# Moving VectorE work between two K stages of a transformer block: query sums earlier, layer-norm statistics on two engines, a block's transposing loads on two queues

## The chip, the cores and the metric

The kernel runs on one core of one Trainium2 chip. The metric is the device time of one execution in microseconds (us). Each of the core's engines has its own instruction queue and works through it strictly in order: TensorE (PE in the profile) multiplies matrices, VectorE (DVE) and ScalarE (ACT) do elementwise work, GpSimd (POOL) does small elementwise work and issues some DMAs, and SyncE (SP) issues DMAs only. An instruction waits at the head of its queue until what it needs is there, and all that stands behind it waits too.

## The reference, cut to what matters

```python
def phi(t): return where(t > 0, t + 1, exp(t)) + 1e-6

mod = (silu(c) @ w_mod)                   # six rows of 512: sa, ca, ga, sb, cb, gb
h = layernorm(x) * (1 + ca) + sa          # x: 2048 x 512
q, k, v = split(h @ wqkv)                 # 32 heads of 16
pq, pk = phi(q), phi(k)
kv, z = pk^T v, sum of pk                 # per head
x = x + ga * ((pq kv / (pq z + 1e-6)) @ wo)
h = layernorm(x) * (1 + cb) + sb
x = x + gb * (mish(h @ w1 + b1) @ w2)     # 512 -> 1792 -> 512
```

All is float32. Everything in this study happens in the second and third line of it: the layer norm of x, its transposition, and the keys.

## The kernel before

**Tiling.** The 2048 rows are four blocks of 512 (b = 0 to 3), and a block is four tiles of 128 x 512. A float32 operand is multiplied as two rounded parts, a high half and a low half (`split`, L80): ScalarE copies the value to the high half, one tick later VectorE subtracts it from the value and gets the low half. `mm3` (L74) is then three matmuls (high x high, high x low, low x high, L76 to L78).

**Normalised and transposed x.** TensorE needs h with the model dimension on the partitions. Blocks 0 and 1 are transposed by TensorE. Blocks 2 and 3 (`TURNED`) go another way: `ln_turned` (L487) normalises the four tiles in place and writes them to DRAM (`to_dram`); `load_squares` (L256) reads them back in small pieces of 32 floats, 16 DMAs a block, four for each tile `y_x`, so that squares of 32 x 32 lie in the right place; VectorE transposes within the squares (`turn`, L267), ScalarE applies scale and shift of the modulation (L269), and `split` makes `hT`. In `ln_turned`, a tile's mean and variance come either from ScalarE (`act_sums`, L221: two passes with accumulation) or from VectorE (`ln_stats`, L192: one statistics and one aggregating operation). Then one power on POOL (L207) gives the reciprocal deviations of all four tiles, VectorE makes the shifts (L237), and each tile is normalised (L216 on ScalarE, L218 on VectorE).

**Keys.** For each block b there are two loops of four units (L847 and L865). `k_unit(b, t)` makes the keys of one tile of rows: 12 matmuls with `hT` of block b. Its followers (`k_post`, L305) take the exponential and the ReLU on ScalarE, join them on VectorE (`ku`, L303), and split them (`pk`). For blocks 1 and 2 a POOL DMA also adds `ku` onto the tile of block 0 (L312), for block 3 VectorE does (L310). `xn_split` splits the normalised tile. `g_unit(b, t)` multiplies it with `pk` into `gacc`, again 12 matmuls. The stage of the "second K" is that of b = 1. The prediction calls these units K1.0 to K1.3, G1.0 to G1.3, K2.0 and so on. After G3.2 comes `z` (L359), which sums the joined `ku` tiles.

**Queries.** The queries of blocks 0 and 1 are made later with seven products instead of eight (`q_sevens`). They need sums of the transposed x of these two blocks: `q_right(c)`, c = 0 and 1, does four subtractions on VectorE, two to a step, and splits the four results one after the other; `q_left(c)` does the like with the weights.

**What sets the order.** Nothing is scheduled by a compiler: instructions enter the queues in the order in which the program calls them. Followers are Python generators. `spawn` adds one, and `tick()` (L59), called behind each unit, runs every generator up to its next `yield`, in the order in which they were spawned. Generators given to `spawn_idle` come last in each tick, and only the first `width[0]` of their list take a step; `width[0]` is 2 in this stretch. So whatever a tick puts on VectorE stands ahead of all that a later tick puts there. In the second loop the transposes of `turn_x` are called at t = 1 and t = 2 ahead of the unit and its tick. SBUF tiles of 128 x 512 share 101 slots.

In the kernel before, `ln_turned(2, 2, 2, sp)` is spawned ahead of G0.3 and `ln_turned(3, 4, 1, pool)` (all four tiles' sums on ScalarE, one tile a tick) at K1.1; `q_right(0)` and `q_right(1)` are spawned behind G1.2 and G1.3.

Of the kernel before, what the change touches and what calls it, by code (L numbers as in the profile page):

```python
# [13 lines left out]
P = 128  # L14
# [13 lines left out]
def block_kernel(ctx: ExitStack, tc: tile.TileContext, x, wqkv, wo, w1, b1t, w2, c, wmodt, out):  # L28
    nc = tc.nc
    act, dve, pool, pe, sp = nc.scalar, nc.vector, nc.gpsimd, nc.tensor, nc.sync  # L30
# [9 lines left out]
    def sb(name, dt=F32, shape=(P, 512)):  # L40

        return big.tile(list(shape), dt, tag="T", name=name, bufs=SLOTS)
# [7 lines left out]
    running, fresh, idle_work, width = [], [], [], [2]  # L50

    def spawn(gen):
        fresh.append(iter(gen))

    def spawn_idle(gen):

        idle_work.append(gen)
# [22 lines left out]
    def split(name, t, keep, key, lo_engine=dve, hi_engine=act, plus=None):  # L80

        hi, lo = sb(f"{name}h", F32R, t.shape), sb(f"{name}l", F32R, t.shape)
        if hi_engine is act:
            act.activation(hi, t, AF.Copy)
        else:
            hi_engine.tensor_copy(hi, t)
        if lo_engine is dve:
            yield
        if plus is None:
            lo_engine.tensor_tensor(lo, t, f32(hi), op=ALU.subtract)  # L90
        else:
            dve.scalar_tensor_tensor(lo, t, plus, f32(hi), op0=ALU.add, op1=ALU.subtract)
        keep[key] = hi, lo


    xt, wm, wraw = {}, {}, {}
# [95 lines left out]
    def ln_stats(key, b, j, t):  # L192

        for d, name, shape in (mv, "mv", [P, 4, 2]), (rs, "rs", [P, 4]), (nb, "nb", [P, 4]):
            if (key, b) not in d:
                d[key, b] = cst.tile(shape, F32, tag=name, name=f"{name}_{key}_{b}", bufs=NB)
        st6 = cst.tile([P, 6], F32, tag="st6", name=f"st6_{key}_{b}_{j}", bufs=4)
        dve.bn_stats(st6, t)
        dve.bn_aggr(mv[key, b][:, j, :], st6)

    def ln_eps(key, b, lo=0, hi=4):
        dve.tensor_scalar(rs[key, b][:, lo:hi], mv[key, b][:, lo:hi, 1], EPS, 1.0, op0=ALU.add, op1=ALU.mult)  # L202

    def ln_rstd(key, b, lo=0, hi=4):

        y = rs[key, b][:, lo:hi]
        pool.tensor_tensor(y, y, half[:, lo:hi], op=ALU.pow)  # L207

    def ln_shift(key, b, lo=0, hi=4):

        dve.scalar_tensor_tensor(nb[key, b][:, lo:hi], mv[key, b][:, lo:hi, 0], -1.0, rs[key, b][:, lo:hi],
                                 op0=ALU.mult, op1=ALU.mult)

    def ln_apply(key, b, j, t, dst, engine):
        if engine is act:
            act.activation(dst, t, AF.Identity, bias=nb[key, b][:, j:j + 1], scale=rs[key, b][:, j:j + 1])  # L216
        else:
            engine.tensor_scalar(dst, t, mv[key, b][:, j, 0:1], rs[key, b][:, j:j + 1],  # L218
                                 op0=ALU.subtract, op1=ALU.mult)

    def act_sums(key, b, t, v):  # L221

        if (key, b) not in rs:
            for d, name in (rs, "rs"), (nb, "nb"):
                d[key, b] = cst.tile([P, 4], F32, tag=name, name=f"{name}_{key}_{b}", bufs=NB)
        scrap = sb(f"scrap_{key}_{b}_{t}")
        sums = cst.tile([P, 2], F32, tag="sums", name=f"sums_{key}_{b}_{t}", bufs=6)
        act.activation(scrap, v, AF.Identity, scale=-1.0 / D, accum_out=sums[:, 0:1])
        act.activation(scrap, v, AF.Square, bias=sums[:, 0:1], accum_out=sums[:, 1:2])
        return sums  # L230
# [5 lines left out]
    def sums_shift(key, b, t, sums):  # L236
        dve.tensor_tensor(nb[key, b][:, t:t + 1], sums[:, 0:1], rs[key, b][:, t:t + 1], op=ALU.mult)  # L237
# [4 lines left out]
    nd, yd = {}, {}  # L242
# [6 lines left out]
    def squares(y, d, col):  # L249

        for c in range(4):
            lo = col + 32 * c
            yield (y[32 * c:32 * (c + 1), :].rearrange("q (m r) -> q m r", r=32),
                   d[:, lo:lo + 32].rearrange("(m q) r -> q m r", q=32))

    def load_squares(key, b, order=(0, 2, 1, 3)):  # L256


        for j in order:
            y = yd[key, b, j] = sb(f"y_{key}_{b}_{j}")  # L260
            for sq, rows_ in squares(y, nd[key, b], P * j):
                sp.dma_start(sq, rows_)

    def turn(key, b, j, keep, name, sc0, sh0):

# [120 lines left out]
    def q_right(c):  # L386

        b11, b12, b21, b22 = [hfx.pop((b, k)) for k in (c, c + 2) for b in (0, 1)]
        t = [sb(f"qt_{c}_{i}") for i in range(4)]
        for n, (d, u, v) in enumerate(((t[0], b12, b11), (t[1], b22, t[0]), (t[2], b22, b12), (t[3], b21, t[1]))):  # L390
            dve.tensor_tensor(d, u, v, op=ALU.subtract)
            if n % 2:
                yield
        for i in range(4):
            yield from split(f"qt_{c}_{i}", t[i], qb, (f"t{i + 1}", c))
# [88 lines left out]
                        plus_one(16, 20)  # L484
            yield

    def ln_turned(b, on_act, per, queue):  # L487

        sums = {}
        rest = list(range(on_act, 4))  # L490
        for n in range(max(on_act, len(rest))):
            if n < on_act:
                sums[n] = act_sums("x", b, n, xt["x", b, n])
            if n < len(rest):
                ln_stats("x", b, rest[n], xt["x", b, rest[n]])
            if (n + 1) % per == 0:
                yield
        for n in range(on_act):
            dve.tensor_scalar(rs["x", b][:, n:n + 1], sums[n][:, 1:2], 1.0 / D, EPS, op0=ALU.mult, op1=ALU.add)
        if rest:  # L500
            ln_eps("x", b, on_act, 4)
        ln_rstd("x", b)
        yield
        for n in range(on_act):
            sums_shift("x", b, n, sums[n])
        for pair in (0, 2), (1, 3):
            for j in pair:
                ln_apply("x", b, j, xt["x", b, j], xt["x", b, j], act if j < on_act else dve)
            if per == 1:
                yield  # L510
            for j in pair:
                to_dram("x", b, j, xt["x", b, j], queue)
        if b == 2:
            yield
            load_squares("x", b, range(4))

    def stats(b, t):
        ln_stats("x", b, t, xt["x", b, t])
# [144 lines left out]
        for j in range(4):  # L663
            load_x(b, j)
    g_unit(0, 2)
    spawn(ln_turned(2, 2, 2, sp))
    tick()
    for j in range(4):
        tr = transpose("x", 1, j, 4, 0, "h" if j < 3 else "tp", pool)
# [175 lines left out]
    for b in range(1, NB):  # L845
        last = b == NB - 1
        if b == NB - 2:  # L847
            spawn(mod_side(range(8, 12), 1))
        for t in range(4):
            k_unit(b, t)  # L850
            if b == 1 and t == 1:
                spawn(ln_turned(3, 4, 1, pool))
            if b == 2 and t == 3:
                load_squares("x", 3, range(4))
            if b == NB - 2:
                load_wqkv(0, t)
            if last and t < 2:
                spawn_idle(q_left(t))
            if last and t == 2:
                spawn_idle(early_rows[0])  # L860
            xn_split(b, t)
            tick()
        if last:
            spawn(wo_scale())
        for t in range(4):  # L865
            if b + 1 in TURNED and t in (1, 2):
                for j in (2 * t - 2, 2 * t - 1):
                    tr = turn_x(b + 1, j)
                    next(tr)
                    spawn(tr)  # L870
            elif not last and b + 1 not in TURNED and t % 2 == 0:
                for j in (t, t + 1):
                    tr = transpose("x", b + 1, j, 4, 0, "tp" if j == t else "h")
                    next(tr)
                    spawn(tr)
            g_unit(b, t)
            if b == 1 and t == 2:
                spawn_idle(q_right(0))
            if b == 1 and t == 3:
                spawn_idle(q_right(1))  # L880
            if last:
                load_x(0, t, "r")
                for k in ((0, 1), (2,), (3,), ())[t]:
                    spawn(split(f"wq_{k}", wraw[0, k], wq, k))
                if t == 2:
                    z_unit()
                if t == 3:
                    spawn(z_side())
            if b == NB - 2:
                wv[t] = sb(f"wv_{t}")  # L890
                sp.dma_start(wv[t], wqkv[P * t:P * (t + 1), 1024:1536])
                wos[t] = sb(f"wo_{t}")
                sp.dma_start(wos[t], wo[P * t:P * (t + 1), :])
            tick()
# [196 lines left out]
    order = {8: [(0, 0), (0, 2)], 9: [(0, 1)], 10: [(0, 3), (1, 0)], 11: [(1, 2)], 12: [(1, 1)], 13: [(1, 3)]}  # L1091
    for b in range(1, NB):
        for t in range(4):
            n = 4 * b + t
# [162 lines left out]
    order = [(b, j) for b in (2, 3) for j in (0, 2, 1, 3)]  # L1257
# [306 lines left out]
```

## Time and profile before

| | us |
|---|---|
| median of three runs | 487.3 (486.95 to 488.3) |
| the profiled execution | 487.84 |
| its span, first to last instruction | 486.1 |
| TensorE busy | 477.5 |
| VectorE busy | 382.2 |
| ScalarE busy | 305.9 |
| POOL busy | 148.0 |

The profile is of one execution; its span leaves out what lies around the first and the last instruction. TensorE's granted clock was 1.00 throughout. In the timelines each line has the start, the duration, the engine, the source line, the operation, output and inputs, and in brackets how long the engine had been idle before it and which instruction ended that. Successive instructions of one engine overlap a little, so the distance of two starts, not the duration, is what an operation takes in a row of them.

### The profile page before, as it was taken

What the parts mean: (1) busy time and instruction counts of PE and PEld (TensorE: products, weight loads), DVE (VectorE), ACT (ScalarE), POOL (GpSimd) and SP (SyncE); (2) the same over time, 40 slices, a digit from 0 to 9 for tenths busy, and PEclk for the clock granted to TensorE, in tenths of its full rate; (3) what the DMA queues carried; (4) which work ended last, traced back from release to release, by engine and by line L of the source; (5) the groups of instructions that cost most, each with busy time, mean ns of one, the idle gap of its engine ahead of it and who ended that gap; (6) DMA issues with size and microseconds to landing.
All of it is one profiled execution on the core that took longest, in us unless ns stands there. A gap on an engine that the chain in (4) does not pass through costs nothing.

```text
span 486.1 us, 7325 instructions
## 1 busy us (share of the span) xinstructions
PE 477.5 (98%) x2326; PEld 390.8 (80%) x2326; DVE 382.2 (79%) x740; ACT 305.9 (63%) x554; POOL 148.0 (30%) x248
## 2 busy tenths in 40 slices
PE   7999999999999999999999999999999999999997
PEld 6777767878887888888888888888888888888887
DVE  6976799999799799978777673899644665689993
ACT  6797988765654888748766764684164454668400
POOL 4674321000023105102234433332726410253600
PEclk9999999999999999999999999999999999999999
DMA  8805989343984227289699989979999922499986
GB/s 302 305 1 137 191 214 233 136 133 95 319 209 113 98 56 232 95 255 357 221 319 374 362 209 208 316 229 329 340 384 359 253 58 79 110 179 234 238 127 134
DMA packets 130849, 103.80 MB, mean 214 GB/s; under 512 B 74449, under 2 KB 95961, under 8 KB 130810
## 3 DMA queue, kind: packets, MB, share of 16 engines
q1 hardware_dynamic: 99528, 57.57, 42.4%
q0 software_dynamic: 29024, 45.24, 35.8%
q10 hardware_dynamic: 2258, 0.53, 0.5%
q8 instruction: 18, 0.29, 0.2%
q14 instruction: 21, 0.17, 0.1%
HBM read 65.55 MB, written 35.66 MB: 208 GB/s over the span
## 4 chain that ended last, share of the span: by engine, by line
PE 87%; DVE 5%; DMA 2%; ACT 2%; SPq 2%; issue 1%; POOL 1%; DVEq 0%; ACTq 0%
PE p_a L1151 20%; PE p_s L1151 8%; PE oacc L76 5%; PE oacc L78 5%; PE oacc L77 5%; PE m L77 5%; PE m L76 5%; PE m L78 5%; PE o L76 3%; PE o L78 3%; PE o L77 3%; PE pq_a L409 3%; PE pq L76 2%; PE pq L78 2%; PE pq L77 1%; PE pk L78 1%
## 5 line engine op out<-in xcount | busy, mean ns | idle before, releaser
L207 POOL TENSOR_TENSOR rs_n<-rs_n,half 128x1 f32<-128x1 f32 x16 | 11.0, 687 | 63.0 <-DVE rs_n L202 35.4
L1156 DVE TENSOR_TENSOR cb<-p_s,u 128x512 f32<-128x512 f32 x28 | 19.3, 688 | 12.1 <-ACT u L1192 12.1
L1161 ACT ACTIVATE u<-p_a 128x512 f32<-128x512 f32 x14 | 8.4, 598 | 25.9 <-PE p_a L1151 25.9
L1449 POOL DMA_DIRECT2D wt_m<-w2t x20 | 14.0, 704 | 32.8 <-PE p_a L1151 21.4
L1186 ACT ACTIVATE u<-p_a 128x512 f32<-128x512 f32 x12 | 7.2, 598 | 25.8 <-PE p_a L1151 25.8
L1143 ACT ACTIVATE ub<-cb,b1c 128x512 f32<-128x512 f32 x28 | 20.0, 718 | 4.6 <-DVE cb L1156 4.4
L1192 ACT ACTIVATE u<-p_a 128x512 f32<-128x512 f32 x14 | 8.4, 597 | 16.2 <-PE p_a L1151 15.4
L1156 DVE TENSOR_TENSOR c<-p_a,u 128x512 f32<-128x512 f32 x14 | 9.6, 690 | 8.2 <-PE p_a L1151 7.1
L909 POOL DMA_DIRECT2D rden_d<-rden x2 | 1.4, 720 | 45.2 <-DVE rden L907 45.2
L792 POOL DMA_DIRECT2D w2b<-w2d x20 | 10.6, 537 | 14.4 <-DVE r L1135 4.4
L303 DVE SCALAR_TENSOR_TENSOR ku<-e_k,relu_k 128x512 f32<-128x512 f32 x15 | 10.7, 716 | 4.2 <-ACT relu_k L301 4.2
L786 POOL DMA_DIRECT2D wb<-w2d x14 | 9.9, 712 | 11.8 <-DVE t L764 10.7
L1120 ACT ACTIVATE u<-p_a,b1c 128x512 f32<-128x512 f32 x14 | 9.6, 687 | 5.7 <-PE p_a L1151 5.7
L303 DVE SCALAR_TENSOR_TENSOR q<-e_q,relu_q 128x512 f32<-128x512 f32 x16 | 10.8, 689 | 3.1 <-ACT relu_q L301 3.1
L312 POOL DMA_DIRECT2D ku<-ku x8 | 7.2, 899 | 19.3 <-DVE ku L303 19.3
L216 ACT ACTIVATE x<-x,nb_x,rs_x 128x512 f32<-128x512 f32 x13 | 10.0, 808 | 4.6 <-DVE nb_x L237 3.9
L839 POOL DMA_DIRECT2D a1b<-rd_a x10 | 5.4, 541 | 24.8 <-PE p_a L1151 9.6
L933 DVE TENSOR_TENSOR r<-o,r 128x512 f32<-128x512 f32 x16 | 10.9, 682 | 0.9 <-PE o L78 0.9
L207 POOL TENSOR_TENSOR rs_x<-rs_x,half 128x1 f32<-128x1 f32 (+1 forms) x10 | 7.7, 780 | 12.0 <-DVE rs_x L202 6.0
L921 DVE SCALAR_TENSOR_TENSOR q<-q,rd 128x512 f32<-128x512 f32 x16 | 10.4, 689 | 0.7 <-DMA rd<-rden_d 0.7
L938 POOL DMA_DIRECT2D x1d<-r x8 | 4.4, 549 | 20.9 <-DVE r L933 20.9
L183 DVE SCALAR_TENSOR_TENSOR wm<-wm,sc_row 128x512 f32<-128x512 f32 x16 | 10.6, 681 | 0.0
(1618 smaller groups left out, 1894.0 us busy)
## 6 DMA issues: line engine op xcount, KB each, us to landing
wm<-in_wmodt_dram SPq DMA_DIRECT2D x24, 256.0 KB, 5.5
w2b<-w2d POOLq DMA_DIRECT2D x20, 256.0 KB, 6.4
wt_m<-w2t POOLq DMA_DIRECT2D x20, 256.0 KB, 5.6
r<-in_x_dram SPq DMA_DIRECT2D x16, 256.0 KB, 3.1
x<-in_x_dram SPq DMA_DIRECT2D x15, 256.0 KB, 4.8
w1p<-in_w_dram SPq DMA_DIRECT2D x14, 256.0 KB, 3.7
w2r<-in_w_dram SPq DMA_DIRECT2D x14, 256.0 KB, 5.3
wb<-w2d POOLq DMA_DIRECT2D x14, 256.0 KB, 4.9
```

The costliest lines, as they stand in the source:

```text
L76: pe.matmul(o, st[0], mv[0], start=start, stop=False)
L77: pe.matmul(o, st[0], mv[1], start=False, stop=False)
L78: pe.matmul(o, st[1], mv[0], start=False, stop=stop)
L183: dve.scalar_tensor_tensor(t, t, 1.0, row, op0=ALU.mult, op1=ALU.mult, accum_out=mc[:, i:i + 1])
L207: pool.tensor_tensor(y, y, half[:, lo:hi], op=ALU.pow)
L303: dve.scalar_tensor_tensor(dst, e, 1.0, r, op0=ALU.min, op1=ALU.add)
L409: pe.matmul(p, l, r, start=onto is None and c == 0 and i == 0, stop=c == 1 and i == 2, skip_group_check=onto is not None)
L933: dve.tensor_tensor(r, p, r, op=ALU.add)
L1143: act.activation(u, p, AF.Mish, bias=b1c[:, f:f + 1])
L1151: pe.matmul(p, st, mv, start=onto is None and c == 0 and i == 0, stop=c == 1 and i == 2, skip_group_check=onto is not None)
L1156: dve.tensor_tensor(out, p, u, op=ALU.add)
L1449: pool.dma_start(v, w2t[g][:, :, SUM[name], :])
```

## The change

Four things are changed.

- `load_squares` takes two queues and deals its DMAs out to them in turn. For block 2 these are SP and POOL (8 each), for block 3 both are SP as before.
- `ln_turned` for block 3 is spawned one tick later (K1.2), and takes the sums of two tiles on ScalarE and of two on VectorE, in two ticks where there were four. It normalises tiles 0 and 1 on ScalarE and 2 and 3 on VectorE, where ScalarE did all four. All that follows the sums comes a tick earlier. Block 2 is as it was: the new argument `applied` names the same two tiles.
- `q_right(0)` and `q_right(1)` are spawned at K1.0 and K1.1, ahead of their ticks.
- The width of the idle list is set to 0 at G1.1 and G2.1 and back to 2 at K2.1 and K3.1 (and at K1.1, where it is 2).

```diff
-    def load_squares(key, b, order=(0, 2, 1, 3)):
+    def load_squares(key, b, order=(0, 2, 1, 3), queues=(sp, sp)):
         for j in order:
             y = yd[key, b, j] = sb(f"y_{key}_{b}_{j}")
-            for sq, rows_ in squares(y, nd[key, b], P * j):
-                sp.dma_start(sq, rows_)
+            for n, (sq, rows_) in enumerate(squares(y, nd[key, b], P * j)):
+                queues[n % 2].dma_start(sq, rows_)
...
-    def ln_turned(b, on_act, per, queue):
+    def ln_turned(b, on_act, per, queue, applied):
...
         for n in range(on_act):
             sums_shift("x", b, n, sums[n])
+        for n in applied:
+            if n >= on_act:
+                ln_shift("x", b, n, n + 1)
         for pair in (0, 2), (1, 3):
             for j in pair:
-                ln_apply("x", b, j, xt["x", b, j], xt["x", b, j], act if j < on_act else dve)
+                ln_apply("x", b, j, xt["x", b, j], xt["x", b, j], act if j in applied else dve)
...
         if b == 2:
             yield
-            load_squares("x", b, range(4))
+            load_squares("x", b, range(4), (sp, pool))
...
-    spawn(ln_turned(2, 2, 2, sp))
+    spawn(ln_turned(2, 2, 2, sp, (0, 1)))
...
             k_unit(b, t)
-            if b == 1 and t == 1:
-                spawn(ln_turned(3, 4, 1, pool))
+            if t == 1:
+                width[0] = 2
+            if b == 1 and t < 2:
+                spawn_idle(q_right(t))
+            if b == 1 and t == 2:
+                spawn(ln_turned(3, 2, 1, pool, (0, 1)))
...
             if b + 1 in TURNED and t in (1, 2):
+                width[0] = 0
...
             g_unit(b, t)
-            if b == 1 and t == 2:
-                spawn_idle(q_right(0))
-            if b == 1 and t == 3:
-                spawn_idle(q_right(1))
```

## The prediction, made before the changed kernel was run

> **What bounds the kernel now.** First the page's head: TensorE is busy 477.5 of 486.1 us, so a change off TensorE can win only its few gaps.
>
> ```profile
> span 486.1 us, 7325 instructions
> PE 477.5 (98%) x2326; PEld 390.8 (80%) x2326; DVE 382.2 (79%) x740; ACT 305.9 (63%) x554; POOL 148.0 (30%) x248
> ```
>
> Then TensorE's timeline from 28 us on; the bracket gives the idle time and who ended it. K1.t and G1.t are the units `k_unit(1, t)` and `g_unit(1, t)`, and so on.
>
> ```profile
> 53.70 0.39 PE L77 MATMUL gacc<-pk_2l,xn_2h 128*128 128x512 f32 x1
> ...
> 56.19 0.39 PE L76 MATMUL gacc<-pk_3h,xn_3h 128*128 128x512 f32 x1
> 56.55 0.50 PE L77 MATMUL gacc<-pk_3l,xn_3h 128*128 128x512 f32 x1
> ...
> 59.18 0.39 PE L76 MATMUL pk<-wk_0h,hT_x_0h 128*128 128x512 f32 x1
> ...
> 61.59 0.50 PE L76 MATMUL pk<-wk_2h,hT_x_2h 128*128 128x512 f32 x1 [0.90 <-ACT hT_x_2h L84]
> ...
> 64.03 0.39 PE L76 MATMUL pk<-wk_0h,hT_x_0h 128*128 128x512 f32 x1
> ...
> 80.38 0.39 PE L76 MATMUL gacc<-pk_3h,xn_3h 128*128 128x512 f32 x1
> 81.96 0.50 PE L77 MATMUL gacc<-pk_3l,xn_3h 128*128 128x512 f32 x1 [1.20 <-DVE pk_3l L92]
> ...
> 84.61 0.39 PE L76 MATMUL pk<-wk_0h,hT_x_0h 128*128 128x512 f32 x1
> 103.93 1.07 PE L359 MATMUL z<-ku,ones 128*32 128x512 f32 x8
> ```
>
> From 64.03 to 80.38 stand 72 matmuls without a gap: 0.227 us each, 2.73 for a unit of 12. So K2.0 (59.18 to 64.03) loses 2.12 us, G2.3 (80.38 to 84.61) loses 1.50 and G1.3 (56.19 to 59.18) 0.26. The first two, 3.6 us in all, are what the change can win. The third matters more: G1.3 is already met with no slack.
>
> Third, the windows, for VectorE on both sides of 60 us:
>
> ```profile
> 42.40:54.40 12.00, 12.00 (x55) 9.94 (x54) 7.18 (x12) 11.63 (x28) 2.83 (x3) 1.00 0.97 188
> 46.00:56.00 10.00, 10.00 (x46) 8.29 (x45) 6.11 (x14) 9.90 (x25) 1.54 (x3) 1.00 1.02 159
> 63.50:84.80 21.30, 20.10 (x87) 16.17 (x87) 21.20 (x40) 17.66 (x33) 4.56 (x6) 1.00 0.94 211
> ```
>
> The columns after the length are PE, PEld, DVE, ACT and POOL busy, the clock, the DMA share and GB/s. VectorE is full from 63.5 to 84.8 (21.20 of 21.30) and has 4.8 us free from 42.4 to 54.4 (7.18 of 12.00). The change carries work from the first stretch into the second.
>
> **The change, part by part.** I walk VectorE's queue in its new order, with these durations:
>
> ```profile
> 32.00 0.69 DVE L198 BATCH_NORM_STATS2 st_x<-x 128x6 f32<-128x512 f32 x1
> ...
> 32.82 0.66 DVE L198 BATCH_NORM_STATS2 st_x<-x 128x6 f32<-128x512 f32 x1
> ...
> 39.84 1.00 DVE L218 TENSOR_SCALAR x<-x,mv_x,rs_x 128x512 f32<-128x512 f32 x2
> 42.41 0.69 DVE L303 SCALAR_TENSOR_TENSOR ku<-e_k,relu_k 128x512 f32<-128x512 f32 x1 [1.57 <-ACT relu_k L301]
> ...
> 54.38 1.30 DVE L267 STREAM_TRANSPOSE hf_x<-y_x 128x512 f32<-128x512 f32 x2
> ...
> 55.81 0.69 DVE L92 SCALAR_TENSOR_TENSOR pk_3l<-ku,pk_3h 128x512 fp32r<-128x512 f32 x1
> ...
> 65.55 0.69 DVE L391 TENSOR_TENSOR qt<-hf_x,qt 128x512 f32<-128x512 f32 x1
> 66.15 0.69 DVE L391 TENSOR_TENSOR qt<-hf_x,hf_x 128x512 f32<-128x512 f32 x1
> ```
>
> A 512-wide operation takes 0.60 in a row of them (65.55 to 66.15), one tile's statistics 0.82 (32.00 to 32.82), an apply 0.50, a transpose 0.61.
>
> *Sums for the turned queries* (`q_right`, idle generators, last in every tick). The tick behind K1.0 gets 2 subtractions, which fit ahead of `ku` at 42.41. K1.1 gets 4, K1.2 gets 2, and the low halves follow, 1 at K1.3 and 2 at G1.0. Between 42.41 and pk_3l stand 6 subtractions and 3 low halves more: 9 x 0.60 = 5.4, and 0.2 for one subtraction that needs the one before it.
>
> *Fourth block's statistics.* Two tiles go to VectorE: 2 x 0.82 = 1.64 at K1.2 and K1.3. The shifts, small, and one apply (0.50) come at G1.1, ahead of pk_3l in the same tick, since the generator was spawned before that `k_post`. So 5.6 + 1.64 + about 0.5 = 7.7 us enter ahead of pk_3l, and only 4.8 are free, of which a gap in front of `ku` of tile 3 stays. Placed one by one, at 0.60 unless named: K1.1, from 42.41, `ku`, xn_0l, 4 subtractions (one of 0.8), to 46.2. K1.2: pk_0l, `ku`, xn_1l, statistics (0.82), 2 subtractions, to 50.0. K1.3: pk_1l, `ku`, statistics, xn_2l, a low half, to 53.3. G1.0: pk_2l, three small ones, then `ku` of tile 3 only at 54.6, since ScalarE has its ReLU done only then (behind the second tile's sums, 52.06 to 53.53), xn_3l, 2 low halves, to 57.0. G1.1: two transposes to 58.25, shift and apply, and **pk_3l starts at 58.9 in place of 55.81** and is done at 59.6.
>
> ScalarE loses two tiles' sums and two applies, and gets the first high halves earlier:
>
> ```profile
> 44.63 0.63 ACT L228 ACTIVATE scrap_x<-x 128x512 f32<-128x512 f32 x1
> ...
> 46.10 0.62 ACT L84 ACTIVATE xn_1h<-x 128x512 fp32r<-128x512 f32 x1
> ...
> 58.64 1.52 ACT L216 ACTIVATE x<-x,nb_x,rs_x 128x512 f32<-128x512 f32 x2 [0.25 <-DVE nb_x L237]
> 60.07 0.81 ACT L269 ACTIVATE hf_x<-hf_x,mc 128x512 f32<-128x512 f32 x1
> 60.91 0.63 ACT L84 ACTIVATE hT_x_2h<-hf_x 128x512 fp32r<-128x512 f32 x1
> 61.45 0.80 ACT L269 ACTIVATE hf_x<-hf_x,mc 128x512 f32<-128x512 f32 x1
> ```
>
> Sums cost 1.47 a tile (44.63 to 46.10), an apply 0.72, a scale and its high half 0.84 + 0.54. So 2 x 1.47 + 2 x 0.72 = 4.4 us leave ScalarE; that buys nothing where TensorE waits for VectorE.
>
> Now TensorE's units. G1.2: pk_2l comes behind a low half, done 53.95 where 53.70 was free: 0.3 lost. G1.3: pk_3h sits behind a high half on ScalarE, done 56.7: 0.25. Then pk_3l at 59.6 where 57.0 would do: 2.6. K2.0 starts at 62.2, 3.0 later than 59.18. Its operands: ScalarE's first apply waits for the shift, which stands on VectorE behind the two transposes (58.4); then apply, two scales, two halves, apply, scale give hT_2h at 64.1 and hT_3h at 65.5, its low half at 66.2. K2.0 would want hT_2h at 63.6, so it still loses 1.5 over these four operands and 0.2 for the restarts (a first matmul behind a wait lasts 0.50, not 0.39), and K2.1 starts at 66.6: **2.55 later** than 64.03. The loss has moved ahead into G1.3.
>
> After that the gain comes. From K2.1 on VectorE holds 5 low halves of `q_right` and none of the 8 subtractions; pk_3l of the third block is done at 81.1, two us before TensorE asks (83.1), and the 1.50 of G2.3 is gone. K3.0 starts at 66.6 + 7 x 2.73 = 85.7 in place of 84.61: 2.55 - 1.50 = **+1.05**.
>
> *The idle width* is 0 from G2.1 to K3.0, so `q_left(0)` is later by a tick and its four sums fall behind `ku`:
>
> ```profile
> 86.67 0.42 DVE L378 TENSOR_TENSOR qs<-wr,wr 128x256 f32<-128x256 f32 x1
> ...
> 88.68 0.69 DVE L303 SCALAR_TENSOR_TENSOR ku<-e_k,relu_k 128x512 f32<-128x512 f32 x1 [0.47 <-ACT relu_k L301]
> ...
> 102.19 0.69 DVE L310 TENSOR_TENSOR ku<-ku,ku 128x512 f32<-128x512 f32 x1
> ```
>
> They took 1.54 (86.67 to 88.21). The last add would end 1.54 after 102.88, at 104.4; `z` starts at 103.93 but reads that tile in its last quarter, at 104.7. Cost 0, at most 0.5.
>
> *Squares by two queues.* This has the one unknown price: POOL issuing a square of 512 pieces of 128 bytes.
>
> ```profile
> L786 POOL DMA_DIRECT2D wb<-w2d x14 | 9.9, 712 | 11.8 <-DVE t L764 10.7 <-DMA a1b<-rd_a 0.6 <-DVE r L1135 0.3
> ...
> L312 POOL DMA_DIRECT2D ku<-ku x8 | 7.2, 899 | 19.3 <-DVE ku L303 19.3
> ...
> L207 POOL TENSOR_TENSOR rs_x<-rs_x,half 128x4 f32<-128x4 f32 x2 | 2.9, 1432 | 4.4 <-DVE rs_x L499 4.4
> L247 POOL DMA_DIRECT2D xd<-x x4 | 2.2, 557 | 4.7 <-ACT x L216 4.4 <-issue 0.2
> ```
>
> 128 pieces cost 0.557 (xd), 256 cost 0.712 (wb): linear, 512 cost 1.02. If pieces cost nothing, 0.56; if they cost as in the accumulating transfer (0.899, taken as 256), 1.59. I take 1.02, nearest to wb, a plain transfer with halved pieces. Eight start with SP's, at 44.9, and end at 53.1. Behind them queue three accumulations of `ku` (0.9 each, 55.8) and the power of the fourth block (1.43, 57.2). VectorE asks for it at 58.25, so the queue is hidden with 1 us to spare: cost 0.
>
> ```profile
> 57.85 0.71 DVE L267 STREAM_TRANSPOSE hf_x<-y_x 128x512 f32<-128x512 f32 x1 [0.73 <-DMA y_x<-xd]
> ```
>
> ```profile
> 44.88 10.48 SPq L262 DMA_DIRECT2D y_x<-xd  x16
> 55.45 0.43 SPq L109 DMA_DIRECT2D wr<-in_wqkv_dram  x1
> ```
>
> The gain is 0 too. SP's 16 took 10.48, and the last tile made the fourth transpose wait until 57.85; but now the first two reach VectorE at 57.0 and the last two at 59.5 and 60.1, behind its own work. The Trainium skill (DMA: Bandwidth & Descriptors, Issuing engines are not separate DMA queues) says that a second issuing queue saves only issue time, since all run on the same 16 engines. The trace leans to it: the share was 1.02 from 46 to 56 with SP alone. By the rule the squares land no earlier; that is rival D.
>
> The view of waits shows no compute engine held by a buffer in this stretch, so I count the earlier claims on the 101 shared slots at 0.
>
> **Sum.** +1.05 at K3.0 and 0 from the other parts. The profiled execution took 487.84 (span 486.1 and 1.74 around it), giving 488.9; it lies 0.5 above the median, 487.3, on which I put the same step: **488.3**.
>
> **Rivals.**
>
> *B, POOL's queue decides (slower).* If a square costs POOL more than 1.15, the power ends after 58.25, and pk_3l, behind the shifts on VectorE, moves by 8 x (price - 1.15). At 1.59 that is 3.5: 491.8. For it: the accumulating transfer. Against: wb.
>
> *C, VectorE absorbs the work (faster).* If most of the 4.8 free us can be used and pk_3l comes by about 57, both losses go: 487.3 - 3.6 = 483.7, or 485 with half of the late gain eaten. Against: 7.7 us do not fit in 4.8, and G1.3 has no slack.
>
> *D, the two queues don't do what they say.* The DMA engines are full, and SP, free at about 50, issues the loads that stood at 55.45 between POOL's squares. Six of 256 KB at the 188 to 211 GB/s of the windows above are 7 to 8 us of DMA. A half of that ahead of the last squares moves their landing from 57.85 to 61.7, behind the transposes at 59.5 and 60.1, and the low halves of hT 0 and 1 queue behind those. Since hT_3h sets the end of K2.0 (ScalarE reaches its scale at 64.0), little shows until 62; a landing at 62.5 costs 0.6: 488.3 to 488.9.
>
> **Chances.** About 0.3% (1.46 us) is what a measurement here can tell from no change: faster below 485.84, slower above 488.76. Forecast (487.3 to 489.3, for half a microsecond in each of the two sums): 0.52, of it 0.41 same, 0.09 slower, 0.02 faster. B 0.27: 0.25 slower, 0.02 same. C 0.13: 0.12 faster, 0.01 same. D 0.08: 0.03 slower, 0.05 same. Together 0.14 faster, 0.49 same, 0.37 slower. The range leaves out C and the last part of B: 486.8 to 491.2.
>
> **What would show it.** pk_3l of block 1 on VectorE near 58.9, and TensorE's longest wait of the stretch, 2 to 3 us, at G1.3 for it; K2.1 near 66.6; no wait at G2.3; the power on POOL over by 58. A power that VectorE's shift waits for means B; G1.3 unhurt means C; the third or fourth transpose waiting for y_x means D. The forecast is wrong if VectorE does the nine moved operations at another pace, or if `z` or the queries after it wait.

## The result, and the profile after

The changed kernel takes 490.26 us (median of five, 489.83 to 491.7), against 487.3 for the kernel before on the same chip. The ratio is 1.0062, 95% interval 1.0041 to 1.0083: 3.0 us slower. The profiled execution took 490.26, with a span of 488.5, 2.4 more than before.

First the head of the page of after. The matmuls are the same 2326, yet TensorE's busy time grew as much as the span: the ends of matmuls are modelled, so the head doesn't show where time was lost, and the waits must.

```profile
span 488.5 us, 7315 instructions
PE 479.9 (98%) x2326; PEld 391.7 (80%) x2326; DVE 384.1 (79%) x743; ACT 301.5 (62%) x544; POOL 153.7 (31%) x256
```

The view of waits of after, TensorE from 42 to 135 us (columns: total, times, longest). Before, two waits stood there: 1.2 for pk_3l, at G2.3, and 0.9 for hT_2h.

```profile
PE gacc L77 <- DVE pk_3l L92: 2.3, 1, 2.3
PE pk L76 <- ACT hT_x_2h L84: 0.4, 1, 0.4
PE pq_s L409 <- DVE cq L420: 0.4, 1, 0.4
PE pq_a L409 <- ACT qu L427: 0.3, 1, 0.3
```

TensorE's timeline of after says where they lie:

```profile
56.37 0.49 PE L76 MATMUL gacc<-pk_3h,xn_3h 128*128 128x512 f32 x1
59.20 0.50 PE L77 MATMUL gacc<-pk_3l,xn_3h 128*128 128x512 f32 x1 [2.34 <-DVE pk_3l L92]
...
61.83 0.39 PE L76 MATMUL pk<-wk_0h,hT_x_0h 128*128 128x512 f32 x1
...
63.75 0.50 PE L76 MATMUL pk<-wk_2h,hT_x_2h 128*128 128x512 f32 x1 [0.40 <-ACT hT_x_2h L84]
...
66.18 0.40 PE L76 MATMUL pk<-wk_0h,hT_x_0h 128*128 128x512 f32 x1
...
85.27 0.39 PE L76 MATMUL pk<-wk_0h,hT_x_0h 128*128 128x512 f32 x1
...
104.55 1.71 PE L359 MATMUL z<-ku,ones 128*32 128x512 f32 x8
...
120.87 0.50 PE L409 MATMUL pq_a<-qt_3h,wq_2h 128*128 128x512 f32 x1 [0.28 <-ACT qu L427]
...
126.98 0.50 PE L409 MATMUL pq_s<-hT_x_2h,qs_0h 128*128 128x512 f32 x1 [0.36 <-DVE cq L420]
```

The wait of 1.20 for the third block's pk_3l, at G2.3, is gone, and one of 2.34 for the second block's stands at G1.3. From K2.1 (66.18) to K3.0 (85.27) nothing waits: 19.09 us, seven units of 2.73. New are a longer `z` (1.71 for 1.07) and two waits in the queries.

VectorE's timeline of after, ahead of both places. Its apply at K1.0 starts at 39.53 here and at 39.84 before; that row is the common zero from here on.

```profile
39.53 1.00 DVE L218 TENSOR_SCALAR x<-x,mv_x,rs_x 128x512 f32<-128x512 f32 x2
...
56.68 1.30 DVE L267 STREAM_TRANSPOSE hf_x<-y_x 128x512 f32<-128x512 f32 x2
57.90 0.19 DVE L237 TENSOR_TENSOR nb_x<-sums_x,rs_x 128x1 f32<-128x1 f32 x2
58.01 0.54 DVE L218 TENSOR_SCALAR x<-x,mv_x,rs_x 128x512 f32<-128x512 f32 x1
58.46 0.68 DVE L92 SCALAR_TENSOR_TENSOR pk_3l<-ku,pk_3h 128x512 fp32r<-128x512 f32 x1
...
80.16 0.69 DVE L92 SCALAR_TENSOR_TENSOR pk_3l<-ku,pk_3h 128x512 fp32r<-128x512 f32 x1
...
89.31 0.69 DVE L303 SCALAR_TENSOR_TENSOR ku<-e_k,relu_k 128x512 f32<-128x512 f32 x1 [3.88 <-ACT relu_k L301]
...
90.52 0.42 DVE L378 TENSOR_TENSOR qs<-wr,wr 128x256 f32<-128x256 f32 x1
...
104.47 0.69 DVE L310 TENSOR_TENSOR ku<-ku,ku 128x512 f32<-128x512 f32 x1
```

The order ahead of pk_3l (58.46) is the one that the prediction walked. Behind K3.0, VectorE idles 3.88 us ahead of `ku`; in the kernel before, the four sums of `q_left(0)` lay in that place (from 86.67). Now they follow `ku`, and the last add onto the key tile ends at 105.16, after `z` wanted to start.

The windows of after, in the order in which those of before were shown:

```profile
42.40:54.40 12.00, 11.95 (x53) 9.57 (x52) 11.38 (x24) 9.48 (x22) 8.72 (x12) 1.00 0.94 173
46.00:56.00 10.00, 9.95 (x44) 7.91 (x43) 9.42 (x20) 8.76 (x20) 9.17 (x13) 1.00 1.12 176
63.50:84.80 21.30, 20.90 (x88) 16.47 (x89) 18.41 (x35) 17.18 (x30) 3.67 (x5) 1.00 0.92 206
```

From 42.4 to 54.4, where VectorE had 4.8 us free, 0.6 are left (11.38 of 12.00); from 63.5 to 84.8, where it was full, 2.9 are free. With two queues, the DMA share from 46 to 56 is 1.12 and the rate 176 GB/s (1.02 and 159 before).

### The profile page after: what moved, and what is told of

The parts are those of the page before. It is cut to its first block, busy times and chain, and to the rows that moved or that the text cites. A ratio compares the mean times of both kernels' runs of the same rounds, so it can differ in the third digit from the quotient of the medians.

```text
span 488.5 us, 7315 instructions
## 1 busy us (share of the span) xinstructions
PE 479.9 (98%) x2326; PEld 391.7 (80%) x2326; DVE 384.1 (79%) x743; ACT 301.5 (62%) x544; POOL 153.7 (31%) x256
## 4 chain that ended last, share of the span: by engine, by line
PE 84%; DVE 8%; ACT 5%; POOL 1%; issue 1%; ACTq 0%; DVEq 0%
PE p_a L1155 19%; PE p_s L1155 8%; PE oacc L78 5%; PE oacc L77 5%; PE oacc L76 5%; PE m L78 5%; PE m L77 5%; PE m L76 5%; PE o L76 3%; PE o L78 3%; PE o L77 3%; PE pq L76 2%; PE pq L78 1%; PE pq L77 1%; PE pk L78 1%; PE pk L76 1%
## 5 line engine op out<-in xcount | busy, mean ns | idle before, releaser
L300 ACT ACTIVATE e_k<-pk 128x512 f32<-128x512 f32 x15 | 8.8, 587 | 5.1 <-PE pk L78 5.1
L216 ACT ACTIVATE x<-x,nb_x,rs_x 128x512 f32<-128x512 f32 x11 | 8.6, 808 | 4.7 <-DVE nb_x L237 4.4
L183 DVE SCALAR_TENSOR_TENSOR wm<-wm,sc_row 128x512 f32<-128x512 f32 x16 | 10.5, 678 | 0.0
```

The source lines that it names most:

```text
L183: dve.scalar_tensor_tensor(t, t, 1.0, row, op0=ALU.mult, op1=ALU.mult, accum_out=mc[:, i:i + 1])
```

## The experiments

Theory: the first sum (+1.05 at K3.0) holds, and the rest of the 3.0 comes from the idle width of 0 in the third block, which moves `q_left`'s and the next sums out of VectorE's free places and pushes its queue through `z` and the queries. Rivals: the POOL queue; squares that land late; the sums alone, or the statistics alone, as the whole cause.

All kernels ran beside the kernel before, whose medians were 487.28 (e1 to e4), 487.7 (e5 to e8), 487.66 (e9, e10), 487.47 (e11) and 487.56 (e12). The table gives, from each profile, by how much the first matmul of a unit is later than before, both counted from the common zero. In before, these stand at 24.19 (K2.1), 44.77 (K3.0), 47.52 (K3.1) and 90.73 (the first query product behind the seven, `pq<-hT_x_0h`, at 130.57 on the clock of the trace). Read along a line, a step shows the place of a loss. The last columns are medians and ratios with 95% intervals. Up to G2.2 the kernel of e2 is the kernel before, and its profile has K2.1 at -0.39: by so much two profiles of the same instructions can differ, so the table serves for steps along a line, and a shift of up to 0.4 that a whole line has in common says nothing.

| kernel | K2.1 | K3.0 | K3.1 | pq | us | ratio |
|---|---|---|---|---|---|---|
| after | +2.46 | +0.97 | +0.94 | +2.71 | 490.26 | 1.0062 (1.0041 to 1.0083) |
| e1 no hold in block 3 | +2.46 | +0.94 | +0.91 | +0.94 | 488.69 | 1.0024 (1.0014 to 1.0034) |
| e2 that hold alone | -0.39 | -0.40 | -0.37 | +1.38 | 489.0 | 1.0034 (1.0022 to 1.0047) |
| e3 sums alone | +3.15 | +1.67 | +2.34 | +2.34 | 489.56 | 1.0041 (1.0027 to 1.0055) |
| e4 statistics alone | +0.40 | +0.28 | +0.33 | +0.34 | 488.13 | 1.0017 (1.0007 to 1.0027) |
| e5 two queues alone | -0.38 | -0.37 | -0.35 | -0.38 | 487.26 | 0.9995 (0.9986 to 1.0003) |
| e6 after, SP alone | +2.43 | +0.92 | +0.89 | +2.63 | 490.01 | 1.0054 (1.0042 to 1.0066) |
| e8 statistics and queues | -0.98 | -0.99 | -0.58 | -0.56 | 486.87 | 0.9985 (0.9977 to 0.9994) |
| e7 sums split | -1.70 | -3.24 | +1.60 | +1.64 | 488.45 | 1.0024 (1.0007 to 1.0040) |
| e9 e7, loads later | -1.70 | -3.24 | -1.44 | -1.44 | 486.54 | 0.9977 (0.9964 to 0.9989) |
| e10 e8, sums split | -0.61 | -2.12 | -0.62 | -0.58 | 487.05 | 0.9988 (0.9973 to 1.0004) |
| e11 e9, side work later | -1.72 | -3.26 | -2.93 | +1.70 | 489.27 | 1.0031 (1.0021 to 1.0040) |
| e12 e11, scalings later | -1.72 | -3.26 | -3.29 | -0.53 | 488.22 | 1.0005 (0.9991 to 1.0019) |

### e1_no_g2_hold

```diff
-                width[0] = 0
+                if b == 1:
+                    width[0] = 0
```

> The changed kernel with the idle width set to 0 only for the second K (from G1.1 to K2.1) and left at 2 from G2.1 on. Theory (the first step of the sum is right, and the second loss comes from the idle width that is 0 from G2.1 to K3.0): q_left(0) makes its sums in the free stretch of VectorE ahead of K3.0 again, z lasts about 1.07 us and not 1.71, the queries behind it do not wait, and 1.4 to 1.8 us of the 2.96 come back: 488.4 to 488.9. Rival (the later waits follow from the shifted statistics and query sums): z and the queries wait as before, 490 us.

Measured: 488.69, as the theory has it. `z` is short again, both waits in the queries are gone, and the shift stays at +0.94 from K3.0 on. The one wait left is the first sum's. Behind it TensorE ran at half clock for about 3.4 us (last section), and lost nothing by it: K2.1 stands at +2.46, as in after. The wait:

```profile
58.70 0.50 PE L77 MATMUL gacc<-pk_3l,xn_3h 128*128 128x512 f32 x1 [2.35 <-DVE pk_3l L92]
```

### e2_hold_only

```diff
+            if b == 2 and t == 2:
+                width[0] = 0
...
             k_unit(b, t)
+            if last and t == 1:
+                width[0] = 2
```

> The kernel before, with one thing more: the idle width is 0 from G2.2 (where q_right has ended in that kernel) to K3.0. Theory (the idle width alone costs 1.4 to 1.8): 488.6 to 489.1, with a long z and waits in the queries, and no change before K3.0. Rival (it costs only beside the other edits, or at most 0.5, as the prediction had it): 487.3 to 487.8.

Measured: 489.0. Nothing is lost up to `z`; 1.75 us (from -0.37 to +1.38) are lost between K3.1 and the query product. `z` and one of the two waits, from its timeline:

```profile
103.66 1.70 PE L359 MATMUL z<-ku,ones 128*32 128x512 f32 x8
...
119.96 0.50 PE L409 MATMUL pq_a<-qt_3h,wq_2h 128*128 128x512 f32 x1 [0.25 <-ACT qu L427]
```

By the medians e1 costs 1.4 and e2 1.7, together 3.1; after costs 3.0. The two parts add up. By the medians the hold is the larger, but the two intervals overlap.

### e3_sums_early

```diff
             k_unit(b, t)
+            if t == 1:
+                width[0] = 2
+            if b == 1 and t < 2:
+                spawn_idle(q_right(t))
...
             if b + 1 in TURNED and t in (1, 2):
+                if b == 1:
+                    width[0] = 0
...
-            if b == 1 and t == 2:
-                spawn_idle(q_right(0))
-            if b == 1 and t == 3:
-                spawn_idle(q_right(1))
```

> The kernel before with only the query sums moved to K1.0 and K1.1, and the idle width 0 from G1.1 to K2.1. Theory (VectorE's queue ahead of pk_3l of the second K decides, and the sums are the larger part of what enters it): pk_3l ends near 59, G1.2 and G1.3 lose 2.5 to 3 us, the wait at G2.3 is gone, in all 0.5 to 2 us slower than before: 488 to 489.3. Rival (the statistics are what overfills VectorE, the sums alone fit): the wait at G2.3 goes and nothing comes for it, 485.8.

Measured: 489.56, 0.26 above the theory's bound; the rival is refuted. The sums alone do the harm at G1.3, now with two waits, the first through ScalarE:

```profile
57.67 0.50 PE L76 MATMUL gacc<-pk_3h,xn_3h 128*128 128x512 f32 x1 [0.99 <-ACT pk_3h L84]
58.70 0.50 PE L77 MATMUL gacc<-pk_3l,xn_3h 128*128 128x512 f32 x1 [0.52 <-DVE pk_3l L92]
...
86.79 0.50 PE L78 MATMUL pk<-wk_0h,hT_x_0l 128*128 128x512 f32 x1 [0.40 <-DVE hT_x_0l L90]
```

The third row is what the theory lacked: the fourth block's normalization ends later (the last store of xd is issued at 67.26, at 64.62 before). The squares that need it come later, and so does the weight load that stands behind them on SP; in VectorE's timeline the last transpose waits 1.42 for its squares, and L183, directly ahead of hT_0l, 1.34 for that weight tile. So K3.0 waits too, the step from +1.67 to +2.34.

### e4_stats_halved

```diff
-            if b == 1 and t == 1:
-                spawn(ln_turned(3, 4, 1, pool))
+            if b == 1 and t == 2:
+                spawn(ln_turned(3, 2, 1, pool, (0, 1)))
```

> The kernel before with only the fourth block's statistics halved between ScalarE and VectorE and spawned at K1.2. Theory (alone it fits into the free time of VectorE, and one tile less for ScalarE to normalise ahead of hT_2h shortens the wait at K2.0): K2.0 loses about 0.9 instead of 2.1, G2.3 still 1.5, in all 1.0 to 1.5 us faster than before: 485.8 to 486.3. Rival (the statistics on VectorE delay pk_3l of the second K by their 1.6 us): 487.3 to 488.5.

Measured: 488.13. The theory missed: the loss at G1.3 goes, but nothing is won. The number is the rival's, the mechanism is not, for pk_3l is early (54.92). VectorE reaches the fourth transpose before its squares have landed; its timeline, and TensorE's behind it:

```profile
54.92 0.68 DVE L92 SCALAR_TENSOR_TENSOR pk_3l<-ku,pk_3h 128x512 fp32r<-128x512 f32 x1
...
58.64 0.71 DVE L267 STREAM_TRANSPOSE hf_x<-y_x 128x512 f32<-128x512 f32 x1 [2.41 <-DMA y_x<-xd]
```

```profile
60.49 0.50 PE L78 MATMUL pk<-wk_0h,hT_x_0l 128*128 128x512 f32 x1 [1.27 <-DVE hT_x_0l L90]
...
63.09 0.50 PE L78 MATMUL pk<-wk_2h,hT_x_2l 128*128 128x512 f32 x1 [0.95 <-DVE hT_x_2l L90]
```

### e5_two_queues

```diff
-                sp.dma_start(sq, rows_)
+                queues[n % 2].dma_start(sq, rows_)
...
-            load_squares("x", b, range(4))
+            load_squares("x", b, range(4), (sp, pool))
```

> The kernel before with the third block's squares on two queues and nothing else. Theory (the squares' issue was late by no more than the 0.73 us that VectorE's fourth turn waited for, and the wait for pk_3l is made by VectorE's other work): ScalarE's four normalizations begin about 0.25 us earlier, K2.0 gains that much, the wait for pk_3l at G2.3 stays about 1.1, and the time is 487.0 to 487.3. Rival 1 (two queues bring nothing to anything): 487.3 and the turn's wait unchanged. Rival 2 (the squares' issue is what holds the second block): VectorE's turns begin earlier by microseconds and the time is under 486.3.

Measured: 487.26 against 487.7, ratio 0.9995 (0.9986 to 1.0003): not to be told from no change, and the expected size lies inside. In the profile no transpose waits, and the wait for hT_2h is 0.47 in place of 0.90. That this is the second queue's doing is not shown: e2, with all squares on SP, has 0.52 there and the same -0.39 at K2.1.

```profile
60.58 0.50 PE L76 MATMUL pk<-wk_2h,hT_x_2h 128*128 128x512 f32 x1 [0.47 <-ACT hT_x_2h L84]
```

### e6_squares_on_sp

```diff
-            load_squares("x", b, range(4), (sp, pool))
+            load_squares("x", b, range(4))
```

> The changed kernel with the third block's squares all on SP again. Theory (in the changed kernel VectorE reaches the turns only at 56.7 to 59, behind the sums and the statistics, when squares issued by one queue until 55.9 are there but for the last): 490.0 to 490.8, the wait for pk_3l at G1.3 still 2.3 and at most some tenths more at the fourth turn. Rival (the two queues carried the change and hid a loss): 491.5 or more, with a wait for y_x over 1 us ahead of a turn on VectorE.

Measured: 490.01, with after's 2.3 us for pk_3l and no wait for squares. In the changed kernel no gain of the second queue shows.

### e8_stats_and_queues

The edits of e4 and e5 together:

```diff
-                spawn(ln_turned(3, 4, 1, pool))
+                spawn(ln_turned(3, 2, 1, pool, (0, 1)))
...
-                sp.dma_start(sq, rows_)
+                queues[n % 2].dma_start(sq, rows_)
```

> The kernel before with the fourth block's statistics halved at K1.2 and the third block's squares on two queues, the sums where they were. Theory (with VectorE light, one queue's squares were the bound that took the gain of the halved statistics: turns waited 2.4 us for them): VectorE's waits for y_x fall under 0.5 us, K2.0 loses nothing to hT_x_0l, the loss of some 1.1 to 1.5 at G2.3 stays since the sums are still there, and the time is 485.4 to 486.5. Rival (two queues bring nothing even here): about 488, the waits for hT_x_0l and hT_x_2l as in the run with the statistics alone.

Measured: 486.87, faster than before (0.9985, 0.9977 to 0.9994), though 0.4 above the expected range. The mechanism is the theory's: VectorE waits for no squares, K2.0 loses nothing to hT_0l, and G2.3 keeps its wait. Against e4 the second queue is worth 0.3% (1.0017 to 0.9985). What the range lacked is a loss of 0.4 at K3.0 (-0.99 to -0.58).

### e7_split

The edits of e8, but all four normalizations on VectorE, and the sums split:

```diff
             k_unit(b, t)
+            if b == 1 and t == 0:
+                spawn_idle(q_right(0))
             if b == 1 and t == 2:
-                spawn(ln_turned(3, 2, 1, pool, (0, 1)))
+                width[0] = 0
+                spawn(ln_turned(3, 2, 1, pool, ()))
...
-            if b == 1 and t == 2:
-                spawn_idle(q_right(0))
             if b == 1 and t == 3:
+                width[0] = 2
                 spawn_idle(q_right(1))
```

> The kernel before with two queues, the halved statistics at K1.2 with all four of their normalizations on VectorE, q_right's first half (two steps of subtractions and one low half) at K1.0 and K1.1 and its second half where it was at G1.3, none in idle places between K1.2 and G1.3, and no such stop in the third block. Theory (the sums fit if they are spread: half of them in VectorE's free time before pk_3l, half behind it): pk_3l at 55 to 57, no wait of over 0.5 us at G1.3, K2.0 as before or earlier, the wait at G2.3 under 0.5, K3.0 one to two microseconds earlier than before, and the time is 484.5 to 486.5. Rival (half of the sums ahead of pk_3l already costs as much as it saves): 487 to 488.5, a wait for pk_3l of about 1 at G1.3 and none at G2.3.

Measured: 488.45, in runs from 485.82 to 490.95. The time is the rival's, but not by its waits: 0.39 at G1.3, none at G2.3, K3.0 3.24 us earlier than before. Ahead of pk_3l stand the four subtractions of `q_right(0)` and no low half; after has nine operations there behind 42.41. All that was won is lost again in K3.0, which takes 7.59 us (+1.60 less -3.24, and 2.75):

```profile
84.53 0.66 PE L78 MATMUL pk<-wk_0h,hT_x_0l 128*128 128x512 f32 x1 [3.00 <-DVE hT_x_0l L90]
84.99 0.63 PE L76 MATMUL pk<-wk_1h,hT_x_1h 128*128 128x512 f32 x1
```

The wait is 3.00 of the 4.84 that K3.0 loses. Another 1.7 goes behind it: the ten matmuls from 84.53 to the next unit at 88.51 take 3.98, where ten at 0.227 take 2.27. The window shows TensorE's granted clock (0.57) over that stretch:

```profile
84.50:88.50 4.00, 3.97 (x10) 3.16 (x11) 3.21 (x7) 0.00 (x0) 0.00 (x0) 0.57 0.64 237
```

Of the twelve executions of e7, the five with a mean granted clock of 0.999 or 1.0 took 485.82 to 487.98, the seven with 0.996 or less 488.12 to 490.95; the profiled one (489.56, 0.996) is of the latter.

VectorE's timeline shows why TensorE waited: the last transpose waits for the fourth block's squares, and the side work of the modulation stands ahead of hT_0l, waiting for a weight tile.

```profile
80.65 0.71 DVE L267 STREAM_TRANSPOSE hf_x<-y_x 128x512 f32<-128x512 f32 x1 [1.37 <-DMA y_x<-xd]
83.17 0.69 DVE L183 SCALAR_TENSOR_TENSOR wm<-wm,sc_row 128x512 f32<-128x512 f32 x1 [1.81 <-DMA wm<-in_wmodt_dram]
...
83.79 0.69 DVE L90 TENSOR_TENSOR hT_x_0l<-hf_x,hT_x_0h 128x512 fp32r<-128x512 f32 x1
```

The view of DMA issues from 44 to 70 (KB each, us to landing) has the fourth block's stores, which the squares need, of before and of e7:

```profile
xd<-x POOLq DMA_DIRECT2D x4, 256.0 KB, 4.0
```

```profile
xd<-x POOLq DMA_DIRECT2D x4, 256.0 KB, 9.3
```

They are issued earlier (55.7 and 58.4, before 59.8 to 64.6) and land no earlier.

### e9_split_loads_late

```diff
-            if b == 2 and t == 3:
+            if b == 2 and t == 2:
                 load_squares("x", 3, range(4))
...
-    def mod_side(order, per):
+    def mod_side(order, per, late=3):
...
-        for n in range(len(steps) + 3):
+        for n in range(len(steps) + late):
...
-            if n >= 3:
-                for i in steps[n - 3]:
+            if n >= late:
+                for i in steps[n - late]:
...
-            spawn(mod_side(range(8, 12), 1))
+            spawn(mod_side(range(8, 12), 1, 4))
```

> The kernel with the sums split (e7) and two edits against the wait of 3.0 us that it had at K3.0: the next weight tile of the third block's side work (L183) is used one tick later, and SP issues the fourth block's squares ahead of two of the weight loads instead of behind them. Theory (that wait was VectorE held 1.8 us at L183 by a weight tile still in flight, and squares that could only follow xd, whose stores landed after 9.3 us instead of 4.0 because the weight loads ran beside them; the sums as such are right in the split place): the wait for hT_x_0l at K3.0 falls to under 1.3, K3.0's third matmul starts about 2 us earlier than in e7, and the time is 485.0 to 487.0. Rival (the xd stores land as late and the squares set K3.0 alone): a wait of 2 to 3 stays and the time is 487.8 to 489.

Measured: 486.54 (0.9977, 0.9964 to 0.9989), the lowest ratio of all, though its interval overlaps those of e8 and e10; the time is as the theory has it. K3.0 waits 0.85 in place of 3.00, later 0.41 for hT_2l, and the clock stays at 1.00:

```profile
82.01 0.50 PE L78 MATMUL pk<-wk_0h,hT_x_0l 128*128 128x512 f32 x1 [0.85 <-DVE hT_x_0l L90]
```

A part of the difference to e7 is thus the half clock that does not come. This profile is of the shortest execution (485.61), that of e7 of one above its median, so the two differ by more than the medians do. The stores of xd land after 7.4 us, the squares go out ahead of two weight loads. The two edits ran together, so their shares stay open.

### e10_halves

To e8 are added the `q_right` and width edits of e7 and the side work of e9:

```diff
+            if b == 1 and t == 0:
+                spawn_idle(q_right(0))
...
+                width[0] = 0
                 spawn(ln_turned(3, 2, 1, pool, (0, 1)))
...
+                width[0] = 2
                 spawn_idle(q_right(1))
...
-            spawn(mod_side(range(8, 12), 1))
+            spawn(mod_side(range(8, 12), 1, 4))
```

> The kernel with the halved statistics and two queues (e8) with q_right's first half at K1.0 and K1.1, none in idle places from K1.2 to G1.3, the second half at G1.3 as before, and the weight tile of the side work one tick later. Theory (half of the sums fits ahead of pk_3l, and what is left behind it fits ahead of G2.3): the wait at G1.3 under 1, the wait at G2.3 under 0.5 where e8 has 1.2, and the time 485.3 to 486.8. Rival (what half of the sums costs at G1.3 is what it saves at G2.3): 486.9 to 488, the two waits together still 1.2 or more.

Measured: 487.05 (0.9988, 0.9973 to 1.0004), 0.25 above the expected range. TensorE waits for pk_3l neither at G1.3 nor at G2.3, and K3.0 is 2.12 earlier than before; 1.50 of that goes in K3.0 itself, where it waits for another low half:

```profile
85.41 0.50 PE L78 MATMUL pk<-wk_2h,hT_x_2l 128*128 128x512 f32 x1 [0.79 <-DVE hT_x_2l L90]
```

### e11_side_later

One edit to e9:

```diff
-            spawn(mod_side(range(8, 12), 1, 4))
+            spawn(mod_side(range(8, 12), 1, 5))
```

> The kernel before this one (e9) with the side work's weight tile (L183) used yet one tick later. Theory (what K3.0 still loses there, 0.85 and 0.41 us, is VectorE at L183 ahead of the low halves of hT: once waiting 0.85 for a weight tile in flight, once with the operation itself): K3.0 loses under 0.5, and the time is 0.6 to 1.2 below that of e9, 485.2 to 486.0. Rival (behind L183 the low halves wait for ScalarE's high halves or for the squares anyway): within 0.3 of e9, 486.2 to 486.8.

Measured: 489.27, and both theories missed. K3.0 lost little, as the first had it (K3.1 at -2.93), but the row that the side work makes came a tick later too, VectorE stood still for it, and the key sum behind it held `z`, which ran in two pieces, with about 3.4 us of half clock behind the wait:

```profile
101.23 0.69 DVE L686 TENSOR_TENSOR wo<-wo,ga_bc 128x512 f32<-128x512 f32 x1 [3.93 <-DMA ga_bc<-ga_d]
```

```profile
103.79 1.32 PE L359 MATMUL z<-ku,ones 128*32 128x512 f32 x2 [2.16 <-DVE ku L310]
```

The half clock cost some 1.4 more: the first six matmuls behind `z` (105.04 to 107.76) took 2.72 for 1.36.

### e12_rows_later

```diff
-        if last:
-            spawn(wo_scale())
         for t in range(4):
+            if last and t == 1:
+                spawn(wo_scale())
```

> The kernel before this one (e11) with one edit: the four scalings of the output weights (L686), which need the row that the side work makes, begin one tick later (at G3.1 in place of G3.0). Theory (VectorE stood 3.9 us at L686 for that row, and the last key tile's sum, which z reads, stood behind it; z and the queries wait for whatever holds VectorE there): the wait at L686 falls under 0.5, z waits under 0.7 where it waited 2.2, K3.1 stays 2.5 to 3 us earlier than before on the common zero, and the time is 484.4 to 486.6, the upper part if the queries behind z then wait. Rival (the scalings a tick later push VectorE's queue through the queries by as much as they save at z): 487 to 489.

Measured: 488.22 (1.0005, 0.9991 to 1.0019). `z` is in time and K3.1 is 3.29 us earlier than before, but the rival is right: the scaling still waits 2.42 for its row, now behind the last key sum, and the queries pay for what follows. Of the 3.29, 2.76 are gone at pq, most of it here:

```profile
118.37 0.50 PE L409 MATMUL pq_a<-qt_3h,wq_2h 128*128 128x512 f32 x1 [1.75 <-ACT qu L427]
```

## Why the prediction was right and wrong

**The time.** 490.26 lies inside the range (486.8 to 491.2) and 2.0 above the forecast of 488.3; it is a slowdown, to which 0.37 had been given (0.25 of it by rival B), not the "same" of the likeliest case. That it lies inside the range is luck: the forecast's own part ended at 489.3, and what lay above was there for B, whose mechanism did not come.

**The walk of VectorE's queue: right.** pk_3l starts at 58.46, which is 58.77 on the trace of before; the forecast was 58.9. K2.1 is 2.46 later (2.55), G2.3's wait is gone, and K3.0 is 0.97 later (+1.05). e1 leaves the hold out and shows that sum alone: +0.94 from K3.0 on, and 1.4 by the medians (0.7 to 1.7 by the interval). e3 and e8 show that it was the nine operations of `q_right` that did not fit: without them, even with the statistics moved, G1.3 loses nothing.

**The idle width, "cost 0, at most 0.5": this step failed.** It costs 1.7 (e2 alone; after less e1 is 1.6). The time of the last add was forecast well: 104.4, and 105.1 with K3.0's own 0.66 on the trace's clock; it ended at 105.16. What failed is that "`z` reads that tile in its last quarter". The view of one line, L359, shows it, of before and of after (columns: duration min/median/max in ns, first and last start):

```profile
L359 PE MATMUL z<-ku,ones x8: 592/604/617, 103.9 to 104.4; 128*32 128x512 f32 x8
```

```profile
L359 PE MATMUL z<-ku,ones x8: 592/605/618, 104.6 to 105.7; 128*32 128x512 f32 x8
```

In before four of the eight start together, one for each tile, so all four tiles are wanted at the start. In after the last tile's two come only behind the add. Their rows, of before and of after:

```profile
103.93 0.64 PE L359 MATMUL z<-ku,ones 128*32 128x512 f32 x4
```

```profile
105.22 1.04 PE L359 MATMUL z<-ku,ones 128*32 128x512 f32 x2
```

So 0.64 is lost at `z`. The second half of the failure is that the step stopped at `z`. The sums that lay ahead of `zsum` at 104.00 (`early_rows`) now stand behind it, from 109.34, and VectorE's queue is late for the queries: 0.28 and 0.36 in waits, and each restart begins with slower matmuls. Laid matmul by matmul beside before, after falls back at three places only: 0.65 at `z`, 0.43 at the first of these waits and 0.66 at the second, together 1.74, which is the step in the table (from +0.94 to +2.71); e2 falls back at the same three. The prediction had named it among what would make it wrong: "if `z` or the queries after it wait".

**POOL's price, 1.02: mis-sized, without effect.** Eight squares took 5.38, 0.67 each, and POOL's power ended at 54.88, not 57.2. Its timeline in after:

```profile
45.22 5.38 POOL L262 DMA_DIRECT2D y_x<-xd  x8 [5.87 <-PE pk L78]
...
53.84 1.04 POOL L207 TENSOR_TENSOR rs_x<-rs_x,half 128x4 f32<-128x4 f32 x1 [0.19 <-DVE rs_x L202]
```

Rival B is refuted: 1.15 would have been its point.

**Squares by two queues, gain 0: right here.** e6 and after have ratios of 1.0054 and 1.0062, 0.0008 apart, with intervals that overlap almost wholly. Rival D's mechanism, squares that land late, did not come: in after no transpose waits. But "by the rule the squares land no earlier" is wrong as a reading of the rule: issue time is what SP alone was short of, and once VectorE is light (e4 against e8) the second queue is worth 0.3%: counted from the common zero, the fourth transpose of e8 starts 2.3 us earlier than that of e4 and waits for no squares. The Trainium skill (DMA: Bandwidth & Descriptors, Issuing engines are not separate DMA queues) says that a second issuing engine saves the time of initiating; the runs agree, and show that with 16 DMAs in 10.48 us this is not small.

**Rival C: not in this kernel.** G1.3 had no slack, as was said. But e9 shows that a part of C was there to be had, 1.1 us by its ratio: with four subtractions ahead of pk_3l and the other sums behind it, both losses go but for 0.4 at G1.3, and K3.0 is 3.24 earlier, near to C's 3.6. More than half of it (1.80) is lost again in K3.0.

## What to carry to other kernels

An average of free time says nothing of where work fits: place each moved operation in the queue, up to the next operation that the bounding engine asks for. Here small operations of 1.54 us had no price in a free place, and one tick later, in a full place, they cost 1.7, at three later deadlines of that queue: follow a delay until an idle place has taken it up. And a gain won early counts only behind the next stage that has no slack: e7, e11 and e12 had 3.2 us at K3.0 and kept none. A wait can also cost more than its length, when half clock follows it (e7, e11).

## What the runs showed of the hardware

- A long wait of TensorE can be followed by half clock. In e1 (first row) the wait of 2.35 ends at 58.70, and from 59.50 to 62.90 ten matmuls run at a granted clock of 0.51, 0.43 us apart; in the same window after (second row) runs 16 at 1.00, 0.23 apart:

```profile
59.50:62.90 3.40, 3.40 (x10) 2.66 (x9) 2.07 (x4) 3.34 (x6) 1.10 (x3) 0.51 0.95 349
```

```profile
59.50:62.90 3.40, 3.40 (x16) 2.79 (x15) 2.59 (x5) 3.34 (x6) 1.10 (x3) 1.00 0.98 322
```

  Such a stretch lasts about 3.4 us in e1, e3, e7 and e11. The wait in after was as long (2.34) and kept the full clock; what decides was not tested. In e1 the stretch cost nothing, since K2.1 stands at +2.46 in both; in e7 it cost 1.7.
- Matmuls with 32 columns run side by side: eight of 0.60 us in 1.07, four starting together at 103.93 and four 0.45 later. The Trainium skill (TensorEngine Tiling (Array Packing), Key Properties) says that different tiles can work in parallel, and the trace agrees.
- A square of 512 pieces of 128 bytes costs POOL 0.67 to issue (0.557 for a store with 128 rows, 0.712 for `wb`): the price does not follow the pieces. On SP the median was 0.49 both where eight were issued (4.06 in all) and where sixteen were (10.48); the longest of the sixteen took 1.43.
- A transfer issued 4 us earlier can land no earlier: xd took 4.0 us to land in before and 9.3 in e7. The same six weight loads had been issued ahead of it in both, and with four ahead of it (e9) it took 7.4; what slowed it stays open.
